# V tiles of 2 MB, longer rows for wq, x and c as rows, and wide value matmuls in a decode block whose attention reads a 32,768-entry cache

## The chip, the cores and the metric

The kernel runs on one core of one Trainium2 chip. The time is device time in microseconds (us).

A 1 MB tile here is 128 partitions of 8 KB. Nearly everything that the kernel reads is read once, so the loads are the work to watch.

## The reference

One token passes through a block: modulations from `c`, a layernorm, attention with 32 query heads on 8 key/value heads over a cache of 32,768 positions, then a second layernorm and a ReLU feed-forward layer. Cut to what matters:

```python
D, Hq, Hkv, Sk, Dh, Dff = 512, 32, 8, 32768, 128, 1792      # all bf16, one token

mod = (silu(c) @ w_mod).reshape(1, 6, 1, -1)                 # sa, ca, ga, sb, cb, gb
h = layernorm(x) * (1 + ca) + sa
q = (h @ wq).reshape(1, 1, Hq, Dh).transpose(0, 2, 1, 3)
k, v = repeat(k_cache, 4, axis=1), repeat(v_cache, 4, axis=1)  # four query heads share a kv head
p = softmax(einsum('bhqd,bhkd->bhqk', q, k) * Dh ** -0.5)
o = einsum('bhqk,bhkd->bhqd', p, v)
x = x + ga * (o.transpose(0, 2, 1, 3).reshape(1, 1, Hq * Dh) @ wo)
h = layernorm(x) * (1 + cb) + sb
x = x + gb * (maximum(h @ w1, 0) @ w2)
```

The caches are 64 MB each. With wq (4 MB), wo (4 MB), w_mod (3 MB), w1 and w2 (1.75 MB each) that is 142.5 MB of 1,048,576 bytes, the 149.4 million bytes that the profile counts.

## The kernel before

All large loads are issued in one order from one queue (SyncE's). K tiles of 1 MB are turned by VectorE (DVE); TensorE (PE) makes the scores of a kv head ("group") with 64 matmuls 512 columns wide. The softmax follows, and the value product is made two groups later with 256 matmuls only four columns wide. The parts that the change and the argument touch:

```python
const  = ctx.enter_context(tc.tile_pool(name="const", bufs=1))   # all small tiles, laid out first
kpool  = ctx.enter_context(tc.tile_pool(name="kpool", bufs=6))   # then the K buffers, 1 MB each
ktpool = ctx.enter_context(tc.tile_pool(name="ktpool", bufs=4))
# ... opened later: headw (w_mod, wq); after that vpool (6 of 1 MB), wopool, wpool

xT_bf = const.tile([P, KT], BF16)                 # x and c: one element per partition and column
cT_bf = const.tile([P, KT], BF16)
nc.scalar.dma_start(out=cT_bf[:], in_=cT_v)
nc.scalar.dma_start(out=xT_bf[:], in_=xT_v)
# ...
sp_dma(wm_sb[:, :, 0:2 * D], wm_v[:, :, 0:2 * D])
for g in range(Hkv):                              # wq: eight slices, rows of 1 KB
    sp_dma(wq_sb[:, :, g * REP * Dh:(g + 1) * REP * Dh], wq_v[:, :, g * REP * Dh:(g + 1) * REP * Dh])
sp_dma(wm_sb[:, :, 2 * D:6 * D], wm_v[:, :, 2 * D:6 * D])
# ...
def load_v(idx):                                  # V: 1 MB, one row of 8 KB per partition, as K
    g, t = divmod(idx, NT)
    Vsb = late["vpool"].tile([P, 32, Dh], BF16, tag="Vsb")
    sp_dma(Vsb[:], vv[:, g, 32 * t:32 * t + 32, :])
    # ... wo of the group (512 KB) after the second V tile
# order: k x 16, then k, v, k, v, ...
# ...
for jl in range(32):                              # value product, per V tile
    J = 32 * Jt + jl
    G, s, j = J // 128, (J % 128) // 16, J % 16
    col = (16 * G + j) * 32 + 4 * s
    nc.tensor.matmul(oT_ps[:], lhsT=Vsb[:, jl, :], rhs=PT_g[:, col:col + 4],
                     start=(J == 0), stop=(J == NJ - 1))
```

Of the kernel before, what the change touches and what calls it, by code (L numbers as in the profile page):

```python
# [17 lines left out]
def kernel(  # L18
# [29 lines left out]
    NMOD = 6 * KT  # L48

# [7 lines left out]
    xT_v = A_x[0, 0].rearrange("(kt p) -> p kt", p=P)  # L57
    cT_v = c[0].rearrange("(kt p) -> p kt", p=P)

    const = ctx.enter_context(tc.tile_pool(name="const", bufs=1))  # L60
    kpool = ctx.enter_context(tc.tile_pool(name="kpool", bufs=6))
# [15 lines left out]
    def pool_dma(out_ap, in_ap):  # L77
        i = nc.scalar.dma_start(out=out_ap, in_=in_ap)
        tc.stamp_issue_order_token(i.ins, "act_stream")
        return i  # L80
# [9 lines left out]
        out=mask4[:],  # L90
        in_=ident_f[:].rearrange("p (x q) -> p q x", q=4),
        op=ALU.add,
        axis=AX.X,
# [14 lines left out]
    xT_bf = const.tile([P, KT], BF16)  # L108
    cT_bf = const.tile([P, KT], BF16)
    with nc.allow_non_contiguous_dma(reason="tiny transposed loads"):  # L110
        nc.scalar.dma_start(out=cT_bf[:], in_=cT_v)
        nc.scalar.dma_start(out=xT_bf[:], in_=xT_v)

# [3 lines left out]
    hT = const.tile([P, KT], BF16)  # L117

    def layernorm_T(src_T, dst_T, shiftT, scaleT, tagp):
        stat_in = const.tile([P, 2], F32, name=f"stat_in_{tagp}")  # L120
        junk = const.tile([P, KT], F32, name=f"junk_{tagp}")
        nc.vector.reduce_sum(out=stat_in[:, 0:1], in_=src_T, axis=AX.X)
        nc.vector.scalar_tensor_tensor(
            out=junk[:], in0=src_T, scalar=1.0, in1=src_T,
# [4 lines left out]
        mean = const.tile([P, 1], F32, name=f"mean_{tagp}")  # L129
        nc.vector.tensor_scalar(out=mean[:], in0=stat_ps[:, 0:1], scalar1=1.0 / D, scalar2=None, op0=ALU.mult)  # L130
        msq = const.tile([P, 1], F32, name=f"msq_{tagp}")
        nc.vector.tensor_tensor(out=msq[:], in0=mean[:], in1=mean[:], op=ALU.mult)
        var = const.tile([P, 1], F32, name=f"var_{tagp}")
        nc.vector.scalar_tensor_tensor(
            out=var[:], in0=stat_ps[:, 1:2], scalar=1.0 / D, in1=msq[:],
# [3 lines left out]
        nc.scalar.activation(out=std[:], in_=var[:], func=ACT.Sqrt, bias=eps_t[:], scale=1.0)  # L139
# [4 lines left out]
            out=xn[:], in0=src_T, scalar1=mean[:], scalar2=rstd[:],  # L144
# [10 lines left out]
    if True:  # L155
        wm_sb = headw.tile([P, KT, 6 * D], BF16)
        sp_dma(wm_sb[:, :, 0:2 * D], wm_v[:, :, 0:2 * D])
        wq_sb = headw.tile([P, KT, Hq * Dh], BF16)
        for g in range(Hkv):
            sp_dma(wq_sb[:, :, g * REP * Dh:(g + 1) * REP * Dh], wq_v[:, :, g * REP * Dh:(g + 1) * REP * Dh])  # L160
        sp_dma(wm_sb[:, :, 2 * D:6 * D], wm_v[:, :, 2 * D:6 * D])

        e_t = const.tile([P, KT], F32)
        nc.scalar.activation(out=e_t[:], in_=cT_bf[:], func=ACT.Exp, scale=-1.0)
        nc.vector.tensor_scalar(out=e_t[:], in0=e_t[:], scalar1=1.0, scalar2=None, op0=ALU.add)
        sig = const.tile([P, KT], F32)
        nc.vector.reciprocal(out=sig[:], in_=e_t[:])
        siluT = const.tile([P, KT], BF16)
        nc.vector.tensor_tensor(out=siluT[:], in0=cT_bf[:], in1=sig[:], op=ALU.mult)  # L169

        modT_ps = small_ps([P, NMOD], "modT_ps")

        def mod_cols(c0, c1):
            for col in range(c0, c1):
                for kt in range(KT):
                    nc.tensor.matmul(  # L176
                        modT_ps[:, col:col + 1],
                        lhsT=wm_sb[:, kt, col * P:(col + 1) * P],
                        rhs=siluT[:, kt:kt + 1],
                        start=(kt == 0), stop=(kt == KT - 1),  # L180
                    )

        mod_cols(0, 2 * KT)
        nc.vector.tensor_copy(out=modT_sb[:, 0:2 * KT], in_=modT_ps[:, 0:2 * KT])

        layernorm_T(xT_bf[:], hT[:], modT_sb[:, 0:KT], modT_sb[:, KT:2 * KT], "ln1")

        qT_ps = small_ps([P, Hq], "qT_ps")
        for hq in range(Hq):
            for kt in range(KT):  # L190
                nc.tensor.matmul(  # L191
                    qT_ps[:, hq:hq + 1],
                    lhsT=wq_sb[:, kt, hq * Dh:(hq + 1) * Dh],
                    rhs=hT[:, kt:kt + 1],
                    start=(kt == 0), stop=(kt == KT - 1),
                )
        nc.scalar.copy(out=qT_sb[:], in_=qT_ps[:])

        qrep_ps = small_ps([P, 4, Hq], "qrep_ps")
        for hp in range(4):  # L200
            nc.tensor.matmul(qrep_ps[:, hp, :], lhsT=sel[:, hp, :], rhs=qT_sb[:], start=True, stop=True)
        nc.vector.tensor_copy(out=qrep_sb[:], in_=qrep_ps[:])

    def mod_rest():
        modT2_ps = small_ps([P, NMOD], "modT2_ps")
        for col in range(2 * KT, NMOD):
            for kt in range(KT):
                nc.tensor.matmul(  # L208
                    modT2_ps[:, col:col + 1],
                    lhsT=wm_sb[:, kt, col * P:(col + 1) * P],  # L210
                    rhs=siluT[:, kt:kt + 1],
                    start=(kt == 0), stop=(kt == KT - 1),
                )
        nc.scalar.copy(out=modT_sb[:, 2 * KT:NMOD], in_=modT2_ps[:, 2 * KT:NMOD])

# [8 lines left out]
    def open_late_pools():  # L224
        mod_rest()
        headw_cm.__exit__(None, None, None)
        late["vpool"] = ctx.enter_context(tc.tile_pool(name="vpool", bufs=6))
        late["wopool"] = ctx.enter_context(tc.tile_pool(name="wopool", bufs=2))
        wpool = ctx.enter_context(tc.tile_pool(name="wpool", bufs=1))
        late["w1_sb"] = wpool.tile([P, KT, Dff], BF16, name="w1_sb")  # L230
        late["w2_sb"] = wpool.tile([P, FT, D], BF16, name="w2_sb")
# [18 lines left out]
    NT = NJ // 32  # L250
# [10 lines left out]
    def load_v(idx):  # L261
        g, t = divmod(idx, NT)
        Vsb = late["vpool"].tile([P, 32, Dh], BF16, tag="Vsb")
        sp_dma(Vsb[:], vv[:, g, 32 * t:32 * t + 32, :])
        v_tiles[(g, t)] = Vsb
        if t == 1:
# [3 lines left out]

    NKT = Hkv * NT
    KLEAD = min(2 * NT, NKT)
    dma_seq = [("k", i) for i in range(KLEAD)]
    ki, vi = KLEAD, 0
    while ki < NKT:
        dma_seq.append(("k", ki)); ki += 1
        dma_seq.append(("v", vi)); vi += 1
    while vi < NKT:
# [3 lines left out]
    def issue_dmas_until(kind, idx):  # L282
        while dma_pos[0] < len(dma_seq):
            if (kind == "k" and (idx // NT, idx % NT) in k_tiles) or (kind == "v" and (idx // NT, idx % NT) in v_tiles):
                return
# [9 lines left out]
    def scores_and_softmax(g):  # L295
# [5 lines left out]
        for G in range(NG):  # L301
            S_ps = ps_s.tile([P, 512], F32, tag="s")
            for t4 in range(4):
                t = 4 * G + t4
                if g > 0:
                    issue_dmas_until("k", g * NT + t)
# [7 lines left out]
                for sl in range(2):  # L314
                    s = 2 * t4 + sl
                    for hp in range(4):
                        h, par = hp // 2, hp % 2
                        first = (t4 == 0 and sl == 0 and hp == 0)
                        last = (t4 == 3 and sl == 1 and hp == 3)
                        nc.tensor.matmul(  # L320
                            S_ps[:],
                            lhsT=Q[:, hp, s, :],
                            rhs=KTv[:, 16 * sl:16 * sl + 16, h, :, par],
                            start=first, stop=last,
# [14 lines left out]
        if True:  # L339
            m_p = spool.tile([P, 1], F32, tag="m_p")  # L340
            nc.vector.reduce_max(out=m_p[:], in_=m2[:], axis=AX.X)  # L341
            mT_ps = small_ps([1, P], "mT_ps")
            nc.tensor.transpose(out=mT_ps[:], in_=m_p[:], identity=ident_f[:])  # L343
            Mrow = spool.tile([1, 4], F32, tag="Mrow")
            nc.vector.tensor_reduce(
                out=Mrow[:], in_=mT_ps[:].rearrange("o (x q) -> o q x", q=4), op=ALU.max, axis=AX.X,
            )
            mr = Mrow[:]
            Mexp = spool.tile([1, P], F32, tag="Mexp")
            nc.vector.tensor_copy(  # L350
                out=Mexp[:].rearrange("o (x q) -> o x q", q=4),
                in_=AP(mr.tensor, mr.offset, [[mr.ap[0][0], 1], [0, 32], [1, 4]]),
            )
            Mb_ps = small_ps([P, 1], "Mb_ps")
            nc.tensor.matmul(Mb_ps[:], lhsT=Mexp[:], rhs=ident_f[0:1, 0:1], start=True, stop=True)  # L355
            nbias = spool.tile([P, 1], F32, tag="nbias")
            nc.scalar.mul(out=nbias[:], in_=Mb_ps[:], mul=-scale)  # L357
            P_g = spool.tile([P, NG * 512], BF16, tag="P_g")
            l_g = spool.tile([P, 1], F32, tag="l_g")
            nc.scalar.activation(  # L360
                out=P_g[:], in_=S_g[:].rearrange("p g f -> p (g f)"), func=ACT.Exp,
                bias=nbias[:], scale=scale, accum_out=l_g[:],
            )
            PT_g = spool.tile([P, NG * 512], BF16, tag="PT_g", bufs=4)
            nc.vector.transpose(out=PT_g[:], in_=P_g[:])  # L365
# [124 lines left out]
```

## Time and profile before

| | before |
|---|---|
| median of 12 runs | 375.73 us (375.6 to 375.82) |
| span in the profile | 373.9 us |
| loads | 149.43 MB, 408 to 424 GB/s in nearly every slice |
| start of the work on the first K tile / on the last load (w2) | 28.28 us / 368.59 us |

These are lines of the page of the kernel before: busy time of the engines; the span in 40 slices (granted PE clock, the share of its full speed that PE was allowed, in tenths; busy share of the 16 DMA engines in tenths, GB/s); the DMA queues (packets, MB, share of 16 engines); the shares of the chain that ended last (a q after an engine's name is its instruction queue); groups of instructions (count, then busy us and mean ns of one, then the idle time before them and what ended it); and loads (count, KB each, us from issue to landing).

```profile
PE 240.6 (64%) x3076; PEld 134.3 (36%) x3076; DVE 178.3 (48%) x185; ACT 27.8 (7%) x67; POOL 8.6 (2%) x14
...
PEclk9999998978695769759875678558785766655555
DMA  7999999999999999999999999999999999999991
GB/s 225 351 417 420 421 423 422 408 418 421 422 417 408 424 419 419 410 419 422 419 422 409 422 418 419 411 418 418 424 413 415 419 421 414 411 421 410 416 364 63
...
q1 hardware_dynamic: 30274, 149.43, 98.4%
q8 instruction: 24, 0.39, 0.4%
q10 hardware_dynamic: 1056, 0.00, 0.2%
...
DMA 85%; DVE 5%; SPq 4%; PE 3%; ACT 1%; issue 1%; DVEq 0%
...
L320 PE MATMUL S_ps<-KTt,qbd 128*128 128x512 bf16 x512 | 170.4, 474 | 72.8 <-DVE KTt L309 72.7
L309 DVE STREAM_TRANSPOSE KTt<-Ksb 128x2048 f32<-128x2048 f32 x64 | 146.4, 2299 | 54.6 <-DMA Ksb<-in_A_k_cache_dram 54.3
...
L392 PE MATMUL oT_ps<-PT_g,Vsb 128*128 128x4 bf16 x2048 | 63.2, 166 | 18.9 <-DMA Vsb<-in_A_v_cache_dram 18.9
...
Ksb<-in_A_k_cache_dram SPq DMA_DIRECT2D x64, 1024.0 KB, 18.9
Vsb<-in_A_v_cache_dram SPq DMA_DIRECT2D x64, 1024.0 KB, 19.8
wq_sb<-in_A_wq_dram SPq DMA_DIRECT2D x8, 512.0 KB, 8.9
```

The DMA row is 9 from the second slice to the last but one, and the chain is 85% DMA. PE (64%) and DVE (48%) wait for loads: DVE's transposes had 54.3 us of idle time that a K landing ended, PE's value matmuls 18.9 us that a V landing ended. So, as I read it, a load that is shorter shortens the kernel, and work on PE is free as long as it stays behind the loads.

The windows view gives the same for two stretches: 30 to 50 us, where only K tiles come, and 100 to 290 us, the steady middle. Columns: stretch, length, busy us (instructions) of PE, its weight loads, DVE, ACT, POOL; granted PE clock; DMA share; GB/s. (A DMA share just over 1 only means that records overlap a little.)

```profile
30.00:50.00 20.00, 16.78 (x64) 6.54 (x64) 18.89 (x11) 0.00 (x0) 0.00 (x0) 1.00 1.01 419
100.00:290.00 190.00, 131.48 (x1531) 69.57 (x1528) 98.88 (x90) 11.77 (x31) 0.00 (x0) 0.72 1.02 417
```

The DMA engines are full in both, at 417 to 419 GB/s.

### The profile page before, as it was taken

Reading aid. Unit: us, or ns where it says so; the run is one execution under the profiler, and the core shown is the slowest. Engines: PE = TensorE matmul, PEld = TensorE weight load, DVE = VectorE, ACT = ScalarE, POOL = GpSimd, SP = SyncE. Lnnn points to the kernel's source line nnn. Section 1 sums busy time; section 2 is a strip of 40 time slices with the busy share of each in tenths; the row PEclk is TensorE's granted clock in tenths of the full one; section 3 lists DMA queues with packets and bytes.
Section 4 is the critical chain, followed back from the end, with each engine's and each line's share of the span. In section 5 each row is a group of like instructions: output and inputs, shape, how many; then the busy total and the mean of one; then the engine's idle time right before and its main releaser. Section 6 shows DMA issues by size and latency. Waiting matters only on the chain.

```text
span 373.9 us, 6797 instructions
## 1 busy us (share of the span) xinstructions
PE 240.6 (64%) x3076; PEld 134.3 (36%) x3076; DVE 178.3 (48%) x185; ACT 27.8 (7%) x67; POOL 8.6 (2%) x14
## 2 busy tenths in 40 slices
PE   0527776867955966675765867676955967643433
PEld 0422332333433524333333434243523533533333
DVE  0209997965545454555435654374445454300020
ACT  1120021110011000200011000200001000200000
POOL 9000000000000000000000000000000000000000
PEclk9999998978695769759875678558785766655555
DMA  7999999999999999999999999999999999999991
GB/s 225 351 417 420 421 423 422 408 418 421 422 417 408 424 419 419 410 419 422 419 422 409 422 418 419 411 418 418 424 413 415 419 421 414 411 421 410 416 364 63
DMA packets 31359, 149.87 MB, mean 401 GB/s; under 512 B 3425, under 2 KB 13410, under 8 KB 14946
## 3 DMA queue, kind: packets, MB, share of 16 engines
q1 hardware_dynamic: 30274, 149.43, 98.4%
q8 instruction: 24, 0.39, 0.4%
q10 hardware_dynamic: 1056, 0.00, 0.2%
q14 instruction: 5, 0.04, 0.0%
HBM read 149.42 MB, written 0.00 MB: 400 GB/s over the span
## 4 chain that ended last, share of the span: by engine, by line
DMA 85%; DVE 5%; SPq 4%; PE 3%; ACT 1%; issue 1%; DVEq 0%
DMA Ksb<-in_A_k_cache_dram 49%; DMA Vsb<-in_A_v_cache_dram 30%; DMA w_sb<-in_B_w_dram 6%; DVE KTt L309 4%; SPq L73 4%; PE S_ps L320 2%; PE oT_ps L392 1%; PE ffnT_ps L443 0%; ACT L360 0%; ACT P_g L360 0%; DVE PT_g L365 0%; DVE S_g L327 0%; PE orow_ps L453 0%; ACT orow_bf L458 0%; PE Mb_ps L355 0%
## 5 line engine op out<-in xcount | busy, mean ns | idle before, releaser
L320 PE MATMUL S_ps<-KTt,qbd 128*128 128x512 bf16 x512 | 170.4, 474 | 72.8 <-DVE KTt L309 72.7
L309 DVE STREAM_TRANSPOSE KTt<-Ksb 128x2048 f32<-128x2048 f32 x64 | 146.4, 2299 | 54.6 <-DMA Ksb<-in_A_k_cache_dram 54.3
L320 PEld LDWEIGHTS <-qbd 128*128 128x128 bf16 x512 | 52.5, 111 | 131.1 <-issue 104.7
L392 PEld LDWEIGHTS <-Vsb 128*128 128x128 bf16 x2048 | 63.8, 102 | 39.7 <-DMA Vsb<-in_A_v_cache_dram 19.9
L392 PE MATMUL oT_ps<-PT_g,Vsb 128*128 128x4 bf16 x2048 | 63.2, 166 | 18.9 <-DMA Vsb<-in_A_v_cache_dram 18.9
L327 DVE TENSOR_SCALAR_CACHE_REDUCE S_g<-S_ps 128x512 f32<-128x512 f32 x16 | 10.9, 684 | 33.8 <-PE S_ps L320 33.8
L397 DVE TENSOR_TENSOR oT_sb<-oT_ps,Linv 128x4 bf16<-128x4 f32 x8 | 1.3, 162 | 47.4 <-PE oT_ps L392 47.4
L248 ACT COPY qbd<-qrep_sb 32x128 bf16<-32x128 bf16 x32 | 9.4, 295 | 178.3 <-PE S_ps L320 177.2
L365 DVE STREAM_TRANSPOSE PT_g<-P_g 128x1024 bf16<-128x1024 bf16 x8 | 10.0, 1245 | 18.5 <-ACT P_g L360 18.5
L355 PEld LDWEIGHTS Mb_ps<-ident_f,Mexp 1*128 1x128 f32 x16 | 3.6, 276 | 17.4 <-DVE Mexp L350 17.0
L360 ACT ACTIVATE P_g<-S_g,nbias 128x1024 bf16<-128x1024 f32 x8 | 9.2, 1148 | 0.2
L357 ACT ACTIVATE nbias<-Mb_ps 128x1 f32<-128x1 f32 x8 | 1.4, 171 | 99.1 <-PE Mb_ps L355 99.1
L369 PEld LDWEIGHTS L_ps<-Lexp,ones_f 128*128 128x128 f32 x16 | 4.6, 308 | 8.4 <-issue 6.6
L369 PE MATMUL L_ps<-Lexp,ones_f 128*128 128x4 f32 x16 | 3.6, 295 | 6.0 <-DVE Lexp L367 6.0
L176 PE MATMUL modT_ps<-siluT,wm_sb 128*128 128x1 bf16 x32 | 1.0, 165 | 9.7 <-DVE siluT L169 9.7
L191 PE MATMUL qT_ps<-hT,wq_sb 128*128 128x1 bf16 x128 | 3.9, 165 | 4.9 <-DVE hT L151 3.5
L343 PE MATMUL mT_ps<-ident_f,m_p 128*1 128x128 f32 x8 | 2.4, 304 | 6.4 <-DVE m_p L341 6.4
L401 PEld LDWEIGHTS <-wo_g 128*128 128x128 bf16 x128 | 4.7, 102 | 3.0 <-issue 2.3
L191 PEld LDWEIGHTS <-wq_sb 128*128 128x128 bf16 x128 | 3.7, 104 | 5.1 <-issue 3.6
L208 PE MATMUL modT_ps<-siluT,wm_sb 128*128 128x1 bf16 x64 | 1.9, 165 | 5.4 <-DMA wm_sb<-in_w_mod_dram 5.4
L371 DVE RECIPROCAL Linv<-L_ps 128x4 f32<-128x4 f32 x8 | 1.4, 173 | 7.5 <-PE L_ps L369 7.5
L401 PE MATMUL attnT_ps<-oT_sb,wo_g 128*128 128x1 bf16 x128 | 4.5, 165 | 0.5 <-DVE oT_sb L397 0.5
(69 smaller groups left out, 49.0 us busy)
## 6 DMA issues: line engine op xcount, KB each, us to landing
Ksb<-in_A_k_cache_dram SPq DMA_DIRECT2D x64, 1024.0 KB, 18.9
Vsb<-in_A_v_cache_dram SPq DMA_DIRECT2D x64, 1024.0 KB, 19.8
wq_sb<-in_A_wq_dram SPq DMA_DIRECT2D x8, 512.0 KB, 8.9
wo_g<-in_A_wo_dram SPq DMA_DIRECT2D x8, 512.0 KB, 18.9
w_sb<-in_B_w_dram SPq DMA_DIRECT2D x2, 1792.0 KB, 21.7
wm_sb<-in_w_mod_dram SPq DMA_DIRECT2D x1, 2048.0 KB, 14.1
wm_sb<-in_w_mod_dram SPq DMA_DIRECT2D x1, 1024.0 KB, 6.1
cT_bf<-in_c_dram ACTq DMA_DIRECT2D x1, 1.0 KB, 6.3
```

Of the source, the lines that this page charges most:

```text
L73: i = nc.sync.dma_start(out=out_ap, in_=in_ap)
L191: nc.tensor.matmul(qT_ps[:, hq:hq + 1], lhsT=wq_sb[:, kt, hq * Dh:(hq + 1) * Dh], rhs=hT[:, kt:kt + 1], start=(kt == 0), stop=(kt == KT - 1),)
L248: nc.scalar.copy(out=o, in_=i)
L309: nc.vector.transpose(out=KTt[:].bitcast(F32), in_=Ksb[:].rearrange("p j d -> p (j d)").bitcast(F32),)
L320: nc.tensor.matmul(S_ps[:], lhsT=Q[:, hp, s, :], rhs=KTv[:, 16 * sl:16 * sl + 16, h, :, par], start=first, stop=last,)
L327: nc.vector.tensor_scalar(out=S_g[:, G, :], in0=S_ps[:], scalar1=1.0, scalar2=None, op0=ALU.mult, op1=ALU.max, accum_out=m2[:, G:G + 1],)
L355: nc.tensor.matmul(Mb_ps[:], lhsT=Mexp[:], rhs=ident_f[0:1, 0:1], start=True, stop=True)
L360: nc.scalar.activation(out=P_g[:], in_=S_g[:].rearrange("p g f -> p (g f)"), func=ACT.Exp, bias=nbias[:], scale=scale, accum_out=l_g[:],)
L365: nc.vector.transpose(out=PT_g[:], in_=P_g[:])
L369: nc.tensor.matmul(L_ps[:], lhsT=ones_f[:], rhs=Lexp[:], start=True, stop=True)
L392: nc.tensor.matmul(oT_ps[:], lhsT=Vsb[:, jl, :], rhs=PT_g[:, col:col + 4], start=(J == 0), stop=(J == NJ - 1),)
L401: nc.tensor.matmul(attnT_ps[:, dc:dc + 1], lhsT=wo_g[:, qh, dc * P:(dc + 1) * P], rhs=oT_sb[:, g, qh:qh + 1], start=False, stop=(g == Hkv ...
```

## The change

Its intent is to spend fewer and longer DMA packets on the same bytes and fewer instructions on the value product. V comes in tiles of 2 MB with rows of 16 KB; wq in four loads with rows of 8 KB instead of eight with rows of 1 KB; x and c as rows, turned by eight small matmuls. For the first six groups the value product has P as the stationary operand and V as the moving one, 512 columns wide; four matmuls against parts of an identity then pick out the diagonal blocks. The last two groups keep the old form, so that the tail does not grow. The diff, cut to its core (left out: a layernorm with two fewer DVE operations, the output sent from ACT's queue, changes of style):

```diff
-    kpool = ctx.enter_context(tc.tile_pool(name="kpool", bufs=6))
+    kpool = ctx.enter_context(tc.tile_pool(name="kpool", bufs=5))
 ...
+    x_row = const.tile([1, D], BF16)
+    c_row = const.tile([1, D], BF16)
+    nc.scalar.dma_start(out=c_row[:], in_=c[0:1, :])
+    nc.scalar.dma_start(out=x_row[:], in_=A_x[0])
 ...
-    xT_bf = const.tile([P, KT], BF16)
-    cT_bf = const.tile([P, KT], BF16)
-        nc.scalar.dma_start(out=cT_bf[:], in_=cT_v)
-        nc.scalar.dma_start(out=xT_bf[:], in_=xT_v)
+    xT = const.tile([P, KT], F32)
+    cT = const.tile([P, KT], F32)
+    for kt in range(KT):
+        nc.tensor.matmul(xcT_ps[:, kt:kt + 1], lhsT=c_row[0:1, kt * P:(kt + 1) * P],
+                         rhs=ident_bf[0:1, 0:1], start=True, stop=True)
 ... (x likewise)
-        for g in range(Hkv):
-            sp_dma(wq_sb[:, :, g * REP * Dh:(g + 1) * REP * Dh], wq_v[:, :, g * REP * Dh:(g + 1) * REP * Dh])
+    for kt in range(KT):
+        sp_dma(wq_sb[:, kt, :], wq_v[:, kt, :])
 ...
-        late["vpool"] = ctx.enter_context(tc.tile_pool(name="vpool", bufs=6))
+        late["vpool"] = ctx.enter_context(tc.tile_pool(name="vpool", bufs=3))
 ...
-        Vsb = late["vpool"].tile([P, 32, Dh], BF16, tag="Vsb")
-        sp_dma(Vsb[:], vv[:, g, 32 * t:32 * t + 32, :])
+        Vsb = late["vpool"].tile([P, 64, Dh], BF16, tag="Vsb")
+        sp_dma(Vsb[:], vv[:, g, 64 * u:64 * u + 64, :])
 ... (order of loads: k, k, v instead of k, v)
+        OLD_FROM = 6
+                if g >= OLD_FROM:
 ... (the old form, 64 matmuls per V tile)
+                else:
+                    for j in range(16):
+                        c0 = (16 * G + j) * 32 + 4 * s0
+                        nc.tensor.matmul(
+                            o_ps[:], lhsT=PT_g[:, c0:c0 + 16],
+                            rhs=Vsb[:].rearrange("p (s j) d -> p s j d", j=16)[:, :, j, :],
+                            start=(u == 0 and j == 0), stop=(u == NU - 1 and j == 15),
+                        )
 ...
+                nc.scalar.copy(out=X[:], in_=o_ps[:])
+                for sp_ in range(4):
+                    nc.tensor.matmul(
+                        oT_ps[:], lhsT=X[:, sp_ * Dh:(sp_ + 1) * Dh], rhs=ident_f[0:16, 4 * sp_:4 * sp_ + 4],
+                        start=(sp_ == 0), stop=(sp_ == 3),
+                    )
```

## The prediction

> **What bounds it now.** The DMA engines. The page's slices show DMA 9+ from 9 to 359 us at 408 to 424 GB/s; the chain of waits is 85% DMA. PE is busy 64%, DVE 48%, both behind the loads. Landings of 1 MB tiles in the trace stand 2.485 us apart all along; packets take 48 ns (1 KB), 164 ns (4 KB), 312 ns (8 KB). From the landing intervals of the 1 MB loads (8 packets per engine), the 512 KB wq loads (32 packets, 1.505 us) and the 2 MB wm load (5.09 us undisturbed) I estimate 9 ns fixed per packet, 23 ns per load, 27.4 B/ns per engine. [...]
>
> **DMA path** (estimates):
> 1. V comes as 32 tiles of 2 MB with 16 KB rows, not 64 of 1 MB with 8 KB rows: 4.875 instead of 4.97 us per 2 MB: -3.0 us, if a 16 KB row is one packet.
> 2. wq comes as four loads of 8 KB rows, not eight of 1 KB rows: 4 x 2.485 instead of 8 x 1.505: -2.1 us.
> 3. x and c come as rows: 1,024 two-byte packets go. While they ran (3.3 to 8.5 us), 2 KB packets came at two thirds of their pace: -1.1 us.
> 4. PE's program shrinks from 6,092 to 3,810 instructions. Its 24 fetches of 16 KB seem to go round eight DMA engines, each setting one back by 1.5 us: the spread of a tile's 16 landings jumps from 0.5 to 2.0 us at 26, to 3.6 at 168, to 5.2 at 296. About 15 fetches mean two hits at most, not three: -1.5 us.
>
> **The engines.** For six groups PV becomes 64 matmuls 512 wide (239 ns at full clock, 427 at half, as the S matmuls show) instead of 256 of 31 ns: 3.8 to 6.8 us per 2 MB instead of 2. With 16 S matmuls PE needs 7.7 us of each 10 us of loads at full clock, 13.7 at half. The clock records hold only 1.0 and 0.5; a busier PE should stay at 1.0 longer ([...]the trace is at 0.5 for good from 321 us, with only V work left). So PE should stay off the critical path. Five K buffers and three V buffers of 2 MB still hold 9 to 10 us of queued loads; the tightest place is the first softmax, where DVE lags about 5 us. The tail after the last V (2 us of matmuls instead of 1) ends before w2 lands: free.
>
> **Sum.** -7.7 us if all holds; I take off 0.6 for gaps and split packets: 368.6 us, 80% range 367.0 to 371.5. Faster by over 2% (below 368.2): 0.40; within 2%: 0.58; slower: 0.02.
>
> **Right if:** V packets of 16 KB near 610 ns, V landings 4.88 us apart; first K landing near 25 us instead of 28.3; about 15 instruction packets, final spread near 3.6 us; PE busy up to 280 us, mean clock above 0.74; no slice under 400 GB/s between 20 and 350 us.
>
> **Wrong if:** 16 KB rows are split (+3 us); PE stuck at half clock, so buffers come free late and the loads show gaps (+2 to +20 us); DVE's lag with five K buffers starves the queue; fetches hit one engine as often as before (+1.5 us).

The sum: 3.0 + 2.1 + 1.1 + 1.5 = 7.7 us off 375.7, with 0.6 put back, came to 368.6 us.

## The result, and the profile after

The changed kernel measured 363.77 us (median of 8 runs, 363.42 to 364.5). The ratio to the kernel before is 0.968, with a 95% interval of 0.9674 to 0.9693: faster by 3.2%. (A ratio is the mean time of one kernel's fast runs over that of the other's of the same rounds, so it is not quite the ratio of the medians quoted.) The gain is 12.0 us; the prediction had 7.1, and the measurement lies 3.2 us below its range.

These are the lines of the page of the kernel after that answer to those of before.

```profile
PE 263.8 (73%) x1980; PEld 124.6 (34%) x1980; DVE 182.9 (50%) x186; ACT 31.3 (9%) x74; POOL 8.7 (2%) x14
...
PEclk9999998999999999899998999899988999855555
DMA  7999999999999999999999999999999999999992
GB/s 298 423 426 427 426 428 425 420 432 430 430 431 423 428 427 423 421 430 431 431 431 422 429 427 429 418 429 430 433 425 425 429 431 422 413 393 425 427 395 90
...
q1 hardware_dynamic: 22016, 149.43, 98.4%
q8 instruction: 15, 0.25, 0.2%
q10 hardware_dynamic: 6, 0.00, 0.0%
...
DMA 76%; DVE 12%; PE 7%; ACT 2%; issue 2%; SPq 1%; DVEq 0%
...
L302 DVE STREAM_TRANSPOSE KTt<-Ksb 128x2048 f32<-128x2048 f32 x64 | 147.0, 2303 | 67.8 <-DMA Ksb<-in_A_k_cache_dram 65.7
L311 PE MATMUL S_ps<-KTt,qbd 128*128 128x512 bf16 x512 | 130.1, 398 | 34.6 <-DVE KTt L302 34.5
L393 PE MATMUL o_ps<-Vsb,PT_g 128*16 128x512 bf16 x384 | 91.9, 395 | 6.5 <-DMA Vsb<-in_A_v_cache_dram 6.5
...
L386 PE MATMUL oT_old<-PT_g,Vsb 128*128 128x4 bf16 x512 | 14.7, 166 | 19.5 <-DMA Vsb<-in_A_v_cache_dram 19.5
...
Vsb<-in_A_v_cache_dram SPq DMA_DIRECT2D x32, 2048.0 KB, 23.5
wq_sb<-in_A_wq_dram SPq DMA_DIRECT2D x4, 1024.0 KB, 10.1
```

The windows view of the kernel after, with the same columns, and with the two stretches around a dip that is discussed below:

```profile
30.00:50.00 20.00, 15.94 (x69) 6.47 (x67) 19.39 (x16) 1.18 (x4) 0.00 (x0) 1.00 1.01 427
100.00:290.00 190.00, 157.04 (x743) 65.94 (x741) 102.43 (x92) 14.66 (x36) 0.00 (x0) 0.96 1.01 427
310.00:320.00 10.00, 7.51 (x163) 5.79 (x161) 0.35 (x2) 1.86 (x2) 0.00 (x0) 0.84 1.00 399
320.00:330.00 10.00, 4.30 (x144) 4.08 (x144) 0.16 (x1) 0.00 (x0) 0.00 (x0) 0.50 0.98 401
```

Most expected effects are there: fewer packets, 15 instruction fetches, a PE that is busier and better clocked and still waits for loads. One thing was not expected. **From 30 to 50 us only K tiles come, by loads that the change does not touch, and they came at 427 GB/s instead of 419.** In the list of packets, the same packets are shorter:

```
median duration of one packet, ns        before                    after
  1 KB (wo, wq, w2)                      48, from 46 to 60        46
  4 KB (second part of w_mod)            164                       159
  8 KB (K)                               312, many at 319          309
 16 KB (V)                               (none)                    611
mean, 30 to 320 us: 1 KB / 8 KB          48.8 / 314.8              46.2 / 309.2
spacing of K landings, 30 to 50 us (us)  2.48 to 2.49              2.43 to 2.45
```

So the packets of the three sizes that both kernels have in this table became shorter, whatever the change did to their loads (those of 2 KB, of the first w_mod load in the first 7 us, kept their median of 84 ns), by these means 2.6 ns at 1 KB and 5.6 ns at 8 KB. Taken as about 4 ns on average, over 1,744 packets per DMA engine before, that is an estimate of 7 us, and no line of the diff says why.

### The profile page after: what moved, and what is told of

It is laid out like the page before. It is cut to its first block, busy times and chain, and to the rows that moved or that the text cites. A ratio compares the mean times of both kernels' runs of the same rounds, so it can differ in the third digit from the quotient of the medians.

```text
span 362.3 us, 4531 instructions
## 1 busy us (share of the span) xinstructions
PE 263.8 (73%) x1980; PEld 124.6 (34%) x1980; DVE 182.9 (50%) x186; ACT 31.3 (9%) x74; POOL 8.7 (2%) x14
## 4 chain that ended last, share of the span: by engine, by line
DMA 76%; DVE 12%; PE 7%; ACT 2%; issue 2%; SPq 1%; DVEq 0%
DMA Ksb<-in_A_k_cache_dram 45%; DMA Vsb<-in_A_v_cache_dram 23%; DVE KTt L302 9%; DMA w_sb<-in_B_w_dram 6%; PE S_ps L311 3%; DMA wq_sb<-in_A_wq_dram 2%; PE oT_old L386 1%; PE o_ps L393 1%; ACT P_g L348 1%; DVE PT_g L353 1%; DVE S_g L316 1%; SPq L73 1%; PE ffnT_ps L453 0%; PE Mb_ps L343 0%; ACT L348 0%
## 5 line engine op out<-in xcount | busy, mean ns | idle before, releaser
L311 PE MATMUL S_ps<-KTt,qbd 128*128 128x512 bf16 x512 | 130.1, 398 | 34.6 <-DVE KTt L302 34.5
L393 PE MATMUL o_ps<-Vsb,PT_g 128*16 128x512 bf16 x384 | 91.9, 395 | 6.5 <-DMA Vsb<-in_A_v_cache_dram 6.5
L311 PEld LDWEIGHTS <-qbd 128*128 128x128 bf16 x512 | 50.4, 100 | 108.0 <-issue 62.5
L393 PEld LDWEIGHTS <-PT_g 128*16 128x16 bf16 x384 | 34.4, 92 | 60.0 <-issue 20.7
L386 PE MATMUL oT_old<-PT_g,Vsb 128*128 128x4 bf16 x512 | 14.7, 166 | 19.5 <-DMA Vsb<-in_A_v_cache_dram 19.5
L386 PEld LDWEIGHTS <-Vsb 128*128 128x128 bf16 x512 | 14.1, 102 | 20.1 <-DMA Vsb<-in_A_v_cache_dram 20.0
L404 PE MATMUL oT_ps<-ident_f,X 16*128 16x4 f32 x48 | 6.3, 250 | 2.1 <-ACT X L401 2.1
L404 PEld LDWEIGHTS oT_ps<-ident_f,X 16*128 16x128 f32 x48 | 5.8, 186 | 2.6 <-ACT X L401 2.6
L343 PE MATMUL Mb_ps<-ident_f,Mexp 1*128 1x1 f32 x16 | 3.0, 256 | 3.7 <-DVE Mexp L338 3.7
L401 ACT COPY X<-o_ps 16x512 f32<-16x512 f32 x6 | 3.5, 576 | 17.5 <-PE o_ps L393 17.5
```

The lines of the kernel that those rows point to most:

```text
L311: nc.tensor.matmul(S_ps[:], lhsT=Q[:, hp, s, :], rhs=KTv[:, 16 * sl:16 * sl + 16, h, :, par], start=(t4 == 0 and sl == 0 and hp == 0), sto ...
L393: nc.tensor.matmul(o_ps[:], lhsT=PT_g[:, c0:c0 + 16], rhs=Vsb[:].rearrange("p (s j) d -> p s j d", j=16)[:, :, j, :], start=(u == 0 and j ...
L404: nc.tensor.matmul(oT_ps[:], lhsT=X[:, sp_ * Dh:(sp_ + 1) * Dh], rhs=ident_f[0:16, 4 * sp_:4 * sp_ + 4], start=(sp_ == 0), stop=(sp_ == 3),)
```

## The experiments

A cause has to change the packets of many loads at once. Three theories came from the diff: that the 1,024 two-byte packets of x and c at the start leave the DMA engines slower for the rest of the run (A); that the many 1 KB packets of wq do (W); that the V loads, with their length and order, set the pace of all (V). A fourth (L) came from the list of addresses of the built programs. In the kernel before, every tile that a load fills (K, V, wq, w_mod, wo, w1, w2) starts at a byte address in the on-chip memory (SBUF) that is 64 past a multiple of 256: the first K buffer at 37,696 = 147 x 256 + 64. In the kernel after all of them start at a multiple of 256: the first K buffer at 39,680 = 155 x 256. The reason is only that the small tiles laid out before them add up to another size. The expectations are quoted as they stood before each run.

### First calls: undo or add one part (e1 to e8)

**e1**: the kernel before, with x and c loaded as rows and turned by PE.

```diff
-        nc.scalar.dma_start(out=cT_bf[:], in_=cT_v)
-        nc.scalar.dma_start(out=xT_bf[:], in_=xT_v)
+    nc.scalar.dma_start(out=c_row[:], in_=c[0:1, :])
+    nc.scalar.dma_start(out=x_row[:], in_=A_x[0])
+    ... eight matmuls against ident_bf[0:1, 0:1], as in the change
```

> The kernel before, with x and c loaded as rows and turned by eight small matmuls; nothing else changed. Theory A (the element-wise loads of x and c leave the DMA engines slower for the whole kernel: in the trace of before 1 KB packets go from 46 to 51 ns and 4 KB packets from 159 to 164 ns once they are done, at 8 us, and 8 KB packets take 312 to 319 ns where the changed kernel shows 309 throughout): 8 KB packets at 309 ns, K landings 2.445 instead of 2.485 us apart, 366.5 to 369 us. Theory B (the pace comes from something else: the 16 KB rows, the wider wq rows, the busier PE): packets stay at 312 ns or more, only the start gains, 374.5 to 375.

Measured: 374.54 us, ratio 0.9968 (0.9952 to 0.9985). The part is worth 1.2 us, as predicted, and the 8 KB packets stayed at 312 ns. Theory A falls.

**e2**: the kernel after, with x and c loaded element by element again.

```diff
-    nc.scalar.dma_start(out=c_row[:], in_=c[0:1, :])
-    nc.scalar.dma_start(out=x_row[:], in_=A_x[0])
-    ... the eight matmuls
+        nc.scalar.dma_start(out=cT[:], in_=c[0].rearrange("(kt p) -> p kt", p=P))
+        nc.scalar.dma_start(out=xT[:], in_=A_x[0, 0].rearrange("(kt p) -> p kt", p=P))
```

> The changed kernel with the old element-wise loads of x and c, nothing else changed back. Theory A: 8 KB packets at 312 ns or more after 8 us, 370 to 373 us. Theory B: packets at 309 ns, about 365 us.

Measured: 366.21 us (365.61 to 369.15), ratio 0.9763 (0.9723 to 0.9802). The two-byte packets are back and the 8 KB packets kept their 309 ns: theory A falls from this side too. The loss of 2.4 us is larger than e1's gain, with a wide spread. The windows view of e2 shows 259 GB/s in the first 10 us, against 310 in the kernel after, and 389 from 60 to 70 us, against 420; why the second stretch is slower was not followed.

**e3**: the kernel before, with the element loads issued from the queue of the large loads.

```diff
-        nc.scalar.dma_start(out=cT_bf[:], in_=cT_v)
-        nc.scalar.dma_start(out=xT_bf[:], in_=xT_v)
+        nc.sync.dma_start(out=cT_bf[:], in_=cT_v)
+        nc.sync.dma_start(out=xT_bf[:], in_=xT_v)
```

> The kernel before with the two element-wise loads issued from SP, on the queue of all other loads, not from ACT. Theory A1 (what slows the engines is that a second queue has been used on all 16 of them): 8 KB packets at 309 ns, 367 to 369 us. Theory A2 (the two-byte packets themselves, whatever the queue): 312 ns or more and 375 to 377 us. Theory B: 375 to 377 us.

Measured: 376.11 us, ratio 1.0011 (0.9996 to 1.0026), slow packets. The queue is not the cause.

**e4**: the kernel after, with the first load of w_mod issued from ACT's queue.

```diff
-    sp_dma(wm_sb[:, :, 0:2 * D], wm_v[:, :, 0:2 * D])
+    nc.scalar.dma_start(out=wm_sb[:, :, 0:2 * D], in_=wm_v[:, :, 0:2 * D])
```

> The changed kernel with one more thing on the ACT queue: the first 1 MB load of w_mod (2 KB packets, 128 partitions, so all 16 engines) is issued from ACT instead of SP. Theory A1 (second queue used on all engines): packets slow down, 8 KB at 312 ns or more, 370 to 373 us. Theory A2 (two-byte packets): 309 ns, 363.5 to 364.5 us. Theory B: 363.5 to 364.5 us.

(That loads into 128 partitions use all 16 engines is read from the kernel after: each of its 112 loads from SyncE's queue leaves 16 landings, and from 30 to 50 us, where only such loads run, the mean busy share of the 16 engines is 1.01.)

Measured: 364.99 us, ratio 0.9711 (0.9697 to 0.9726), fast packets. Neither is which queue starts. The time is 1.2 us above the kernel after and misses the expected 363.5 to 364.5; e4 too is slower from 60 to 70 us (403 GB/s), and why was not followed.

**e5**: the kernel after, with the old value product in all groups.

```diff
-        OLD_FROM = 6
+        OLD_FROM = 0
```

> The changed kernel with the old narrow PV matmuls in all eight groups; loads as changed. Theory F (instruction fetches set DMA engines back): about 24 fetch packets instead of 15, a final landing spread above 3 us, 1.5 to 3 us longer: 365.3 to 367 us. If PV's form has another part in the pace (theory V), 8 KB packets at 312 ns or more and 368 us or longer. PE's clock falls from 0.90 to about 0.75; without effect if PE is off the path.

Measured: 365.09 us, ratio 0.9717 (0.9702 to 0.9731); packets fast (309 ns), clock 0.745, 24 instruction fetches again. The value product as such does not make the packets fast. It is worth 1.3 us, less than the 1.5 to 3 us that I expected. Of the 16 landings of w2's load, the last came 3.8 us after the first, against 1.9 us in the kernel after and 5.1 us before. This does not prove the theory of fetches that set single engines back: with 15 fetches too the spread is 3.2 us in e16, the kernel after once more, and 4.2 us in e4. Fetches alone were not varied, so what makes the 1.3 us is not shown.

**e6**: the kernel after, with each V tile brought by two loads of 8 KB rows.

```diff
-        sp_dma(Vsb[:], vv[:, g, 64 * u:64 * u + 64, :])
+        sp_dma(Vsb[:, 0:32, :], vv[:, g, 64 * u:64 * u + 32, :])
+        sp_dma(Vsb[:, 32:64, :], vv[:, g, 64 * u + 32:64 * u + 64, :])
```

> The changed kernel with each 2 MB V tile filled by two loads of 8 KB rows; tiles, buffers and matmuls stay. Theory W: packets stay at 309 ns, and only the fixed cost per packet and per load comes back, 32 x 0.03 to 0.1 us, so 364.5 to 367 us. Theory V: K packets at 312 ns or more, 368 to 371 us.

Measured: 364.66 us, ratio 0.9704 (0.9688 to 0.9721), packets fast. Theory V falls, and the 16 KB rows are worth 0.9 us, not the 3.0 us of the prediction.

**e7** and **e8**: the four long wq loads put into the kernel before, and the eight short ones into the kernel after.

```diff
# e7 (on the kernel before); e8 is the reverse, on the kernel after
-        for g in range(Hkv):
-            sp_dma(wq_sb[:, :, g * REP * Dh:(g + 1) * REP * Dh], wq_v[:, :, g * REP * Dh:(g + 1) * REP * Dh])
+        for kt in range(KT):
+            sp_dma(wq_sb[:, kt, :], wq_v[:, kt, :])
```

> The kernel before with wq in four loads of 8 KB rows instead of eight of 1 KB rows; nothing else changed. In every run with the slow packets so far they begin near 8 us, while only wq packets move. Theory W (the 1 KB-row loads of wq set the slower pace, and it stays): 8 KB packets at 309 ns all along, K landings 2.445 us apart, 366 to 369 us. Theory V (the pace comes from the V loads or the PV matmuls, and what is seen at 8 us is only the cost of 1 KB rows): K packets still at 312 ns or more, a gain of 2 to 3 us, 373 us.

> The changed kernel with the old eight wq loads of 1 KB rows; nothing else changed back. Theory W: 8 KB packets at 312 ns or more from 8 us on, 369 to 372 us. Theory V: packets at 309 ns once wq is in, 366 us.

Measured: e7 374.09 us, ratio 0.9956 (0.9941 to 0.9971), slow packets; e8 364.86 us, ratio 0.9710 (0.9695 to 0.9724), fast packets, its 1 KB packets of wq at 46 ns. Theory W falls. The part is worth 1.65 us in the kernel before and 1.1 us in the kernel after. (The kernel after itself ran between 363.32 and 364.92 us in twelve runs, e16's four included, so differences from its 363.77 are sure to a few tenths of a us only.)

After eight runs no part of the change as written carries the 4 ns. What does go with them, in all ten kernels, is the start address: 64 past a multiple of 256 in before, e1, e3 and e7, a multiple of 256 in after, e2, e4, e5, e6 and e8.

### Moving the addresses alone (e9, e10, e11)

One unused tile at the head of the small tiles shifts everything behind it. **e9** puts 192 bytes per partition into the kernel before (64 + 192 = 256); **e10** puts 64 bytes into the kernel after; **e11** puts 64 bytes into the kernel before, which brings its tiles to 128 past a multiple of 256.

```diff
     const = ctx.enter_context(tc.tile_pool(name="const", bufs=1))
+    pad = const.tile([P, 96], BF16)        # e9: 192 bytes.  e10, e11: [P, 32], 64 bytes
+    nc.gpsimd.memset(pad[:], 0.0)
```

> The kernel before with one unused tile of 192 bytes per partition put in front of all others in SBUF (and zeroed once); nothing else changed. In the built programs every tile that a load fills starts at 64 modulo 256 bytes in all kernels with slow packets so far, and at 0 modulo 256 in all with fast ones; the padding takes it to 0. Theory L (the start of a packet in SBUF against 256 bytes sets some 5 ns per packet): 8 KB packets at 309 ns, 1 KB at 46, landings of 1 MB tiles 2.445 instead of 2.485 us apart, about 1,500 packets per engine x 5 ns = 6 to 8.7 us less: 367 to 370 us. Theory P (the pace comes from what the changed kernel does otherwise: tile size, buffer counts, order of loads): unchanged, 375.5 to 376.

> The changed kernel with an unused tile of 64 bytes per partition in front, which moves every loaded tile from 0 to 64 modulo 256 bytes; nothing else changed. Theory L: slow packets, 8 KB at 312 ns or more; about 1,250 packets per engine x 5 ns = 6.3 us more: 368.5 to 370.5 us, which is what was predicted for the changed kernel. Theory P: 363.5 to 364.5 us.

> The kernel before with 64 bytes of padding: loaded tiles at 128 modulo 256 bytes. If only multiples of 256 are fast: slow packets, 375 to 376.5 us. If multiples of 128 are enough: 309 ns and the time of the run with 192 bytes of padding. Theory P: 375.5 to 376.

Measured: e9 368.34 us (368.33 to 368.39), ratio 0.9804 (0.9789 to 0.9818); e10 368.85 us (368.79 to 368.94), ratio 0.9816 (0.9800 to 0.9833); e11 375.26 us, ratio 0.9988 (0.9973 to 1.0003). The middle stretch in the windows view, for e9, then e10, then e11, one fence each; the last number is GB/s, against 417 before and 427 after.

```profile
100.00:290.00 190.00, 135.23 (x1573) 71.28 (x1570) 100.86 (x90) 11.77 (x31) 0.00 (x0) 0.71 1.01 424
```

```profile
100.00:290.00 190.00, 155.21 (x732) 64.73 (x731) 100.96 (x92) 14.64 (x36) 0.00 (x0) 0.96 1.01 421
```

```profile
100.00:290.00 190.00, 132.65 (x1537) 69.98 (x1534) 98.65 (x90) 11.78 (x31) 0.00 (x0) 0.71 1.02 418
```

The row of GB/s in the pages of e9 and e10 shows where the shift acts. In e9 every slice is faster than in the kernel before, the second (wq, in packets of 1 KB) included, which went from 351 to 392. In e10 all but three slices are slower than in the kernel after: the first, and the two at 413 and 393 GB/s of the dip discussed below.

```profile
GB/s 229 392 427 427 427 428 424 418 430 425 427 423 419 428 426 425 418 429 427 425 427 418 427 427 424 423 426 425 427 419 427 426 426 419 425 426 418 422 387 69
```

```profile
GB/s 301 413 417 424 418 425 417 411 428 429 427 427 405 423 424 421 413 423 429 430 423 407 427 423 421 409 425 427 431 421 412 426 423 420 421 427 411 421 378 60
```

The packets answer alike (mean over 30 to 320 us, in ns):

```
                                 start mod 256    1 KB    8 KB    16 KB
before                                64          48.8    314.8
before + 192 bytes (e9)                0          46.0    309.8
before + 64 bytes (e11)              128          49.0    314.5
after                                  0          46.2    309.2   614.6
after + 64 bytes (e10)                64          49.0    314.6   616.3
```

The times make a table of two by two (medians in us):

| | tiles at 64 mod 256 | tiles at 0 mod 256 | worth of the start address |
|---|---|---|---|
| code of before | 375.72 | 368.34 (e9) | 7.4 |
| code of after | 368.85 (e10) | 363.77 | 5.1 |
| worth of the change as written | 6.9 | 4.6 | |

The start address is worth 7.4 us in one code and 5.1 in the other, and the packets account for the difference. The recorded durations of the large loads' packets add up, per DMA engine, to 368.1 us before and 360.5 in e9, to 361.0 in e10 and 355.8 in e16, the kernel after once more (356.6 in its first profile, with the dip). With 1,744 packets per engine before and 1,264 after, the times make 4.2 and 4.0 ns per packet on average. And 128 is not enough: e11 is nearly as slow as the kernel before. Theory L holds. The lower left cell is the kernel that I predicted without knowing it: 368.85 against 368.6.

### Is it each packet's own start? (e13, with e16 beside it)

**e13** puts 64 bytes before the K buffers and 192 behind them, so that in the kernel after the K buffers alone start at 64 mod 256. **e16** is the kernel after unaltered.

```diff
     const = ctx.enter_context(tc.tile_pool(name="const", bufs=1))
+    pad_a = ctx.enter_context(tc.tile_pool(name="pad_a", bufs=1)).tile([P, 32], BF16, name="pad_a")
+    nc.gpsimd.memset(pad_a[:], 0.0)
     kpool = ctx.enter_context(tc.tile_pool(name="kpool", bufs=5))
+    pad_b = ctx.enter_context(tc.tile_pool(name="pad_b", bufs=1)).tile([P, 96], BF16, name="pad_b")
+    nc.gpsimd.memset(pad_b[:], 0.0)
```

> The changed kernel with the five K buffers alone moved to 64 modulo 256 bytes (64 bytes of padding before that pool, 192 after it); all other tiles stay at 0. If each packet pays for its own start: K packets (8 KB) at 312 ns or more while V loads, V packets near 611, wo packets at 46 ns once the K phases are over, 512 K packets per engine x 4 to 5 ns = 2 to 2.6 us more than the changed kernel: 365.5 to 366.8. If one misaligned pool slows all packets: 368.5 to 369. If it isn't the loaded tiles' own start: 363.5 to 364.5.

> The changed kernel unaltered, beside the others on the same chip: 363.4 to 364.5 us.

Measured: e13 365.11 us (364.73 to 365.96), ratio 0.9720 (0.9707 to 0.9733); e16 363.96 us (363.32 to 364.92), ratio 0.9688 (0.9675 to 0.9702). The K-only stretch and the middle of e13:

```profile
30.00:50.00 20.00, 15.78 (x66) 6.32 (x65) 19.20 (x13) 1.18 (x4) 0.00 (x0) 1.00 1.01 422
100.00:290.00 190.00, 154.52 (x744) 65.58 (x744) 101.22 (x93) 14.65 (x36) 0.00 (x0) 0.97 1.01 426
```

In the K-only stretch the landings are back at 2.47 to 2.49 us, while the 16 KB packets keep their median of 611 ns and the 1 KB packets their 46. So it is in the main the packets of the shifted tiles that become longer, and a kernel is not put as a whole into a slow mode. But the price is not fixed per packet. The size missed: e13 lost 1.15 us against e16 where I expected 2 to 2.6, over 512 K packets per engine 2.2 ns each, about half of the 4. The packet records show where: K's packets average 313.4 ns from 30 to 50 us, where they are alone, but 310.5 from 100 to 290 us, where V and wo come between them; there 73% of them take 309 ns or less, as aligned ones do, against 7% in the kernel before. Why a shifted packet costs less among aligned ones was not followed.

Two more things about the mechanism stay open. In the kernels with shifted tiles the first packets are recorded at the fast durations until 7 to 10 us (12 us in e7) and slow only after that, though all tiles are shifted alike; in the kernel before the 1 KB packets have a median of 46 ns until 8 us and of 51 to 52 ns from there to 14 us. And 128 costs about as much as 64: 4.0 ns per packet (e11 against e9) and 4.2 ns (before against e9), averages over packets of different cost. So the runs show that tiles at a multiple of 256 are loaded with shorter packets than tiles at 64 or 128 past it (309.8 ns in e9 against 314.8 and 314.5, at 8 KB); why was not shown.

### The dip near 320 us, and a faster version (e12, e14, e15)

The profile of the kernel after has one slice at 393 GB/s, 317 to 326 us; the windows view above shows 399 and 401 for the two stretches. e16, the same kernel, has no such dip in its profiled execution:

```profile
310.00:320.00 10.00, 5.87 (x157) 5.18 (x154) 0.34 (x2) 1.86 (x2) 0.00 (x0) 0.76 1.03 438
320.00:330.00 10.00, 4.30 (x144) 4.08 (x144) 0.16 (x1) 0.00 (x0) 0.00 (x0) 0.50 0.99 416
```

So it belongs to some executions only. In the profiled execution with the dip, the last wide value product fell into a stretch, 307.1 to 310.5 us, in which the PE clock was at half: its 16 matmuls took 5.31 us (3.62 in e16), and the 2 MB V buffer came free that much later. The next V load was issued at 312.25 us, right after them, and in e16 at 310.53. So my reading is that the late buffer makes the dip. **e14** gives that group the old form.

```diff
-        OLD_FROM = 6
+        OLD_FROM = 5
```

> The changed kernel with the narrow PV matmuls from group 5 on instead of 6. The last wide group holds V buffers through the last softmax, and the load rate falls to 393 to 413 GB/s between 308 and 327 us. If that costs time: no slice under 415 there and 0.5 to 1 us less than the changed kernel beside it. If the engines that are behind lose nothing by it: the same within 0.3 us.

Measured: 363.47 us (363.43 to 363.55), ratio 0.9673 (0.9660 to 0.9687): 0.5 us below e16 by the medians (though e16's fastest run, 363.32, is below all of e14's), and the spread of the runs fell from 1.6 to 0.12 us. The stretches of e14:

```profile
310.00:320.00 10.00, 4.13 (x130) 3.99 (x130) 0.97 (x3) 0.70 (x1) 0.00 (x0) 0.50 1.02 434
320.00:330.00 10.00, 4.30 (x144) 4.08 (x144) 0.16 (x1) 0.00 (x0) 0.00 (x0) 0.50 1.01 422
```

The dip is gone, as the reading says, and the V load was issued at 307.64 us; one profile of a dip that comes and goes is weak proof, the narrow spread of all runs a stronger one.

**The tail.** After the last load only the feed-forward matmuls of w2 remain. The timeline of PE in the kernel after (start, us, work, and in brackets the idle time before it and what ended it):

```profile
353.63 1.63 PE L444 MATMUL hidT_ps<-h2T,w_sb 128*128 128x1 bf16 x56 [1.75 <-DVE h2T L155]
356.75 1.66 PE L453 MATMUL ffnT_ps<-hidT,w_sb 128*128 128x1 bf16 x56 [1.49 <-DMA w_sb<-in_B_w_dram]
```

PE waits 1.49 us for w2 and then works 1.66 us. **e12** loads w2 in rows of 7 KB and in two halves, and for that must take w1's columns in steps of 14:

```diff
-    w2_v = B_w2.rearrange("(ft p) d -> p ft d", p=P)
+    w2_v = B_w2.rearrange("(p ft) d -> p ft d", p=P)
...
-    sp_dma(w2_sb[:], w2_v)
+    sp_dma(w2_sb[:, 0:FH, :], w2_v[:, 0:FH, :])
+    sp_dma(w2_sb[:, FH:FT, :], w2_v[:, FH:FT, :])
...
-    lhsT=w1_sb[:, kt, ft * P:(ft + 1) * P]
+    lhsT=w1_sb[:, kt, :].rearrange("k (m f) -> k f m", f=FT)[:, ft, :]
... (the w2 matmuls of the first half before those of the second)
```

> An attempt to beat both: the changed kernel with w2 laid out so that each partition's rows are contiguous (7 KB packets instead of 1 KB; w1's columns taken in steps of 14 to match) and loaded in two halves, the first half's matmuls run before the second half lands. At 9 ns fixed per packet 96 fewer packets per engine give 0.4 to 0.9 us, half the last matmuls about 0.8 us: 362 to 363 us. If the stepped weight loads are slower than 31 ns each they still end before w2 lands.

Measured: 364.83 us (364.14 to 366.39), ratio 0.9716 (0.9692 to 0.9739): nothing gained, and my expectation was wrong. The timeline of e12 says why:

```profile
353.50 3.46 PE L446 MATMUL hidT_ps<-h2T,w_sb 128*128 128x1 bf16 x56 [1.75 <-DVE h2T L155]
...
357.24 1.63 PE L457 MATMUL ffnT_ps<-hidT,w_sb 128*128 128x1 bf16 x56 [0.27 <-ACT hidT L451]
```

With a stepped stationary operand the 56 matmuls took 3.46 us instead of 1.63, 62 ns each instead of 29; the median record of a weight load grew from 104 to 158 ns. The matmuls of w2 start at 357.24 us, and what ended the wait before them is no longer the landing of w2 but ACT's hidden layer, which waited for the 56 slow matmuls. The load was no longer last; PE was.

**e15** keeps w2's layout and only halves its load, on top of e14:

```diff
+    FH = FT // 2
-    sp_dma(w2_sb[:], w2_v)
+    sp_dma(w2_sb[:, 0:FH, :], w2_v[:, 0:FH, :])
+    sp_dma(w2_sb[:, FH:FT, :], w2_v[:, FH:FT, :])
...
+    nc.vector.memset(ffnT_ps[:], 0.0)      # so that both halves may add to it (start=False)
+    for h0, h1 in ((0, FH), (FH, FT)):
+        for dc in range(KT):
+            for ft in range(h0, h1):
```

> As e14, and w2 in its old layout loaded in two halves, the last layer's first 28 matmuls run before the second half lands. The 1.65 us of the last 56 matmuls after the last landing become 0.8: 0.8 us less than e14; 362 to 363.2 us.

Measured: 362.80 us (362.72 to 362.88), ratio 0.9655 (0.9642 to 0.9668). The timeline of e15 shows one half of the work done before the second half of w2 lands:

```profile
354.75 0.88 PE L457 MATMUL ffnT_ps<-hidT,w_sb 128*128 128x1 bf16 x28 [0.27 <-ACT hidT L451]
355.97 0.91 PE L457 MATMUL ffnT_ps<-hidT,w_sb 128*128 128x1 bf16 x28 [0.34 <-DMA w_sb<-in_B_w_dram]
```

This version beats both kernels; 0.7 us of it comes from the tail (363.47 to 362.80).

## Why the prediction was wrong

It said 368.6 us, 367.0 to 371.5; measured were 363.77. The terms of its sum, beside what the runs gave:

| term | predicted | measured | from |
|---|---|---|---|
| start of the load-filled tiles | not in the sum | -7.4 (on before), -5.1 (on after) | e9, e10 |
| V rows of 16 KB | -3.0 | -0.9 with aligned tiles | e6 |
| wq rows of 8 KB | -2.1 | -1.65 (before), -1.1 (after) | e7, e8 |
| x and c as rows | -1.1 | -1.2 (before), -2.4 (after, wide spread) | e1, e2 |
| shorter PE program, wide value product | -1.5 | -1.3 | e5 |

With the start address first, the sum is 7.4 + 0.9 + 1.1 to 1.65 + 1.2 + 1.3 = 11.9 to 12.4 us; measured are 12.0. The parts were measured on different kernels, though, and with e2's 2.4 us for x and c the sum is 13.1: it closes to about 1 us and no better.

**The step that failed** is the prediction's reading "Landings of 1 MB tiles in the trace stand 2.485 us apart all along; packets take 48 ns (1 KB), 164 ns (4 KB), 312 ns (8 KB)", from which it took "9 ns fixed per packet", and on which the sum rests. It treated these as what such packets cost, so that a load which the diff does not touch would keep its pace. In fact about 4 ns per packet, on average, came from where the tiles start, and the change moved every start without a word of it in the diff. Two errors follow. The gain on untouched packets (all of K, w_mod, wo, w1, w2) was missing. And the fixed cost, read from misaligned packets, was too large for the state that the change led to: halving V's packets was priced at 3.0 us and gave 0.9. What halving them gives with misaligned tiles was not run by itself; the whole change gives 6.9 us there (before against e10), where the prediction had 7.1. The packet records point the same way. By their means, two misaligned packets of 8 KB take 2 x 314.8 - 616.3 = 13 ns more than one of 16 KB; two aligned ones, by their medians, 2 x 309 - 611 = 7 ns. Over 256 such pairs per engine these make estimates of 3.4 and 1.8 us, so the predicted 3.0 fitted the state of the trace that it was read from. Why e6 gave 0.9 and not 1.8 stays open. That 368.85 came so near to 368.6 is in part luck: wq was priced at 2.1 us and gave 1.65.

**The range** had its four risks all on the slow side (16 KB rows split, PE at half clock, K buffers, fetches), and "faster by over 2%" had 0.40. None of them came at the size feared: the second showed as the dip near 320 us, which e14 puts at about 0.5 us. So nothing made up for the gain that was missing from the sum.

**Right, point by point.** V packets of 16 KB take 611 ns (said: near 610). V landings, where only V comes, are 4.85 to 4.88 us apart (said: 4.88). 15 fetches (said: about 15). PE busy 263.8 us (said: up to 280) at a mean clock of 0.905 instead of 0.742, off the critical path: DVE and PE together grew from 8 to 19% of the chain but the DMA engines stayed full, at a share of 1.01 in the middle. The estimate that a busier PE keeps its clock held here: the windows view has 0.72 before and 0.96 after for the middle, and with the old value product in the kernel after (e5) the mean of the whole run is 0.745 again.

**Wrong in detail.** The work on the first K tile starts at 24.27 us (said: its landing near 25, from 28.3): 4.0 us gained where 3.3 were expected. The final spread of landings is 1.9 us (said: near 3.6), but 3.2 us in e16, so this one is no clear miss. Slice 36 lies at 393 GB/s (said: none under 400), in the profiled execution, not in all.

**Could it have been seen?** Yes, in part. The kernel before already recorded 1,115 of its 8 KB packets at 309 ns and 3,095 at 319, all of one size. The floor that most of them missed was the sign: in the kernel after 8,695 of 8,704 take 309 ns. And the addresses of both built programs could be compared before anything ran.

## What to carry to other kernels

When loads bound a kernel, look up where the load-filled tiles start and bring them to a multiple of 256 bytes; here an unused tile of 192 bytes was worth 2% of the time (7.4 of 375.7 us, e9), more than any part of the change as written. (Offsets of 0, 64 and 128 were tried, no others.) Before an effect is credited to a change, compare the packets of a load that the change does not touch: if they moved as well, something else moved. A pace read from a trace holds for the state that the trace was in, so look for its floor before carrying it to another program.

## Three costs that the runs measured, and what they left open

- **Cost of a tile's start for loads.** Here SBUF tiles at 64 past a multiple of 256 cost 7.4 us of 375.7 (e9) and 5.1 us of 368.9 (e10), about 4 ns per packet on average, and 128 past it is nearly as slow (375.26 us, e11). Why the first 7 to 12 us do not show it, and why shifted packets among aligned ones mostly do not (e13), is open.
- **What an instruction fetch does to loads.** The profiles count 24 fetches with 6,152 recorded matmuls and weight loads (before), 15 with 3,960 (after): one to 256 and to 264 of them. A fetch of 16 KB is recorded in the DMA engines for 0.88 to 1.12 us in these two. The spread of a tile's 16 landings grew in three steps from 0.5 to 5.1 us before, and to 1.9 us after (3.2 in e16); that fetches cause it was not isolated, and what a fetch costs the loads was not measured.
- **Stepped weight loads.** With columns in steps of 14, 56 matmuls took 3.46 us instead of 1.63, and a weight load 158 ns instead of 104 (e12).
